# Sliding-window attention with two expert layers on one core: a new load order at the start, a new written-out order of twelve steps, and three changes of where work is done

## The chip, the cores and the metric

The kernel runs on one core of one Trainium2 chip. The metric is the device time of one execution in microseconds (us). Of the kernel before three runs were timed: 764.28, 768.56 and 769.66 us; the median is 768.56 us.

## What is computed

Inputs: q, k and v of 4 batches, 8 heads, 576 positions and 64 columns, all float32. Three stages follow each other, on 2304 tokens of 512 columns:

```
scores = q k^T / 8, kept where 0 <= i - j < 64;  x = softmax(scores) v       # attention
h = x @ w_in                               # 512 -> 2048, w_in and w_out are float64 in the input
P = a0 + a1 h + a2 h^2 + a3 h^3;  Q = 1 + |b0| |h| + |b1| h^2
y = (P / (Q + 1e-6)) @ w_out               # 2048 -> 512
e = argmax(y @ w_gate)                     # one of 8 experts per token
out = gate * sigmoid((y @ w_output_gate)[e]) * (relu(y @ w1[e]) @ w2[e])     # 512 -> 1024 -> 512
```

Products are made to near float32 accuracy: each operand is split into a rounded part and a remainder (both fp32r), and three matmuls stand for one.

## The kernel before

**Tiling.** The 2304 tokens are nine blocks of 256. Attention works on units: one block and two heads, 36 units in all. `at_T` transposes k and q of a unit on TensorE (with the identity matrix as one operand), `at_QK` makes the scores, `soften` the softmax (masks on VectorE, exponentials on ScalarE, the scaling on GpSimd), `at_PT` transposes the probabilities, `at_PV` multiplies by the values. The first three blocks do so unit by unit (`group` 1), the other six with two units at a time (`group` 2).

**The rational layer** is 72 steps, a step being one block and 256 of the 2048 columns: `rt_mm1` (24 matmuls of 256 columns, tile `h`), `rt_head`, `rt_inv`, `rt_tail` and `rt_gsplit` (the quotient, on ScalarE, VectorE and GpSimd), and four steps later `rt_mm2` (12 matmuls of 512 columns, tile `y`). The weights come in as 16 transfers of 1 MB (tile `stg`) and are converted from float64 by three VectorE operations a half (`convert`, tiles `cp` and `ct`), a copy and a subtraction.

**Routing.** After a block's last step `rt_y` writes y out, `rt_ytr` transposes it, `rt_logits` multiplies it with the gate columns (`wg`, 32 columns), `rt_logits2` transposes the result, `rt_route` picks the expert and `rt_rank` the row in the expert's list. `post` does one of these in each step.

**Expert slots.** At the end the tokens, sorted by expert, go through slots: four of 512 rows, one of 256, a half slot of 128. For each slot `w_load` brings eight tiles of 1024 columns of the expert's weights (`wr`), `w_split` rounds each (a copy, first half of `wx`) and subtracts (second half of `wx`). `slot` makes tile `hp` (first product), splits its relu into `hT` (ScalarE, then VectorE), transposes the next slot's tokens (`xtp`), and makes tile `yp` (second product).

**What sets the order.** Everything before step 12 is recorded on a tape (class `Tape`), and `play` issues it in the order written in `ORDER`: a number is the place on the tape and the letter the engine (P TensorE, A ScalarE, D VectorE, G GpSimd, S the queue of SyncE). Each engine keeps the order of its own letters. After step 12 the order comes from the tile framework's scheduler, guided by the priorities in `later`. `pick` gives an operation that two engines can do to the one with less charged work (`charge`); `arith` charges a subtraction of 1024 columns on VectorE at three times its estimate. `evs` lists what attention does in each half event.

The start of the tape: `load_qk(0)` issues q (places 2 and 3) and k (4 and 5), then one transfer brings all constants into the tile `KK` (place 6: identity, masks and small tables), then v (7 and 8), then q and k of the second pair of unit pairs (12 to 15), then the first weight tile (16).

```
    qk_upto(0)
    nc.sync.dma_start(out=cs, in_=cst[:, :C_QC + 1])
    v_upto(0)
    qk_upto(1)
    c_load(1)
```

Of the kernel before, what the change touches and what calls it, by code (L numbers as in the profile page):

```python
# [7 lines left out]
F32 = mybir.dt.float32  # L8
# [25 lines left out]

S_TAPE = 12
ORDER = (
# [32 lines left out]
)  # L69


# [58 lines left out]
def kernel(  # L130
# [89 lines left out]
    def pt(shape, name):  # L220
        return ps.tile(shape, F32, tag=name, name=name)

    def f32(ap):
        return ap.bitcast(F32)
# [26 lines left out]
    def evac(o, i, n, mul=None):  # L251
        e = pick(D=dve(n), A=act(n))
        if mul is None:
            nc.either(e, D=lambda: nc.vector.tensor_copy(out=o, in_=i), A=lambda: nc.scalar.copy(out=o, in_=i))
        else:
            nc.either(e, D=lambda: nc.vector.tensor_scalar(out=o, in0=i, scalar1=mul, scalar2=None, op0=ALU.mult),
                      A=lambda: nc.scalar.mul(out=o, in_=i, mul=mul))
# [11 lines left out]
    def mm(o, lhsT, rhs, start, stop):  # L269
        r = nc.tensor.matmul(o, lhsT, rhs, start=start, stop=stop)  # L270
        pe[0] = r and r.ins
# [34 lines left out]
    def runs(t0, n):  # L306
        done = 0
        while done < n:
            b, s = divmod(t0 + done, S)
            step = min(n - done, S - s)  # L310
            yield done, step, b, s
            done += step
# [2 lines left out]

    def load_qk(m):
        u, g = divmod(m, 2)
        for nm, src, dst in (("q", q, q_t), ("k", k, k_t)):
            dst[m] = t2([128, 2, 4, D], nm)
            for t in range(2):  # L320
                for off, n, b, s in runs(u * TB + t * 128, 128):
                    nc.sync.dma_start(
                        out=dst[m][off:off + n, t],
                        in_=src[b, 4 * g:4 * g + 4, s:s + n, :].rearrange("h p d -> p h d"),
                    )

    def load_v(m):
        u, g = divmod(m, 2)
# [289 lines left out]
        yq_t.pop(j, None)  # L618
        ysb_t[j] = ys

    yT_t, lT_t, ob_t = {}, {}, {}

    def rt_ytr(j, t):
        ys = ysb_t[j][t]
# [13 lines left out]

    def rt_logits(j, t):
        yh, yl = yT_t.pop((j, t))  # L640
        lt = pt([4 * E, 128], "lt")
        with in_turn():
            for c in range(KD):
                mm(lt, wg[:, c, :], yh[:, c, :], c == 0, False)
                mm(lt[:2 * E], wg[:, c, :2 * E], yl[:, c, :], False, c == KD - 1)
        ls = sm.tile([4 * E, 128], F32, tag="ls", name="ls")
        evac(ls, lt, 128)
        lT_t[j, t] = ls

    def rt_logits2(j, t):  # L650
        lg = pt([128, 4 * E], "lg")
        with in_turn():
            transpose(lg, lT_t.pop((j, t)))
        if t == 0:
            lg_t[j] = sm.tile([128, 2, 2 * E], F32, tag="lgs", name="lgs")
        charge("D", 0.15)
        nc.vector.tensor_reduce(out=lg_t[j][:, t, :], in_=lg.rearrange("p (x e) -> p e x", x=2), axis=AX.X, op=ALU.add)
# [198 lines left out]
    def w_split(j, x):  # L856
        t = raw_t.pop((j, x))
        w = t8([128, 2, 1024], "wx")
        r = copy(w[:, 0, :], t, 1024)
        if CH[min(j, NPRE - 1)] < NB - 1:  # L860
            tc.keep_in_program_order(r)
        arith(w[:, 1, :], t, f32(w[:, 0, :]), ALU.subtract, 1024)
        wt[j, x] = w

    def gather(j):
# [192 lines left out]
    for n in range(NUNIT + 2):  # L1058
        first, second = [], []
        if n < NUNIT and (group(n) == 1 or n % 2):  # L1060
            first.append((at_QK, n))
        if n + TA < NUNIT:
            second.append((at_T, n + TA))
        while done < min(n, NUNIT) and (group(done) == 1 or n % 2 == 0):
            first.append((at_PT, done))
            if group(done) == 1:
                second.append((at_PV, done))
            done += 1
        if n % 2 and n > 2 and group(n - 2) == 2:
            second.append((at_PV, n - 2))  # L1070
        evs += [first, second]
    assert done == NUNIT

# [20 lines left out]
    nc.on = True  # L1094
    nc.gpsimd.dma_start(out=co[:, 4:6], in_=cb.partition_broadcast(128))
    nc.gpsimd.dma_start(out=co[:, 0:4], in_=ca.partition_broadcast(128))
    qk_upto(0)
    nc.sync.dma_start(out=cs, in_=cst[:, :C_QC + 1])
    v_upto(0)
    qk_upto(1)  # L1100
    c_load(1)
# [24 lines left out]
    def post(j, r):  # L1126
        if r == 0:
            rt_ytr(j, 0)
        elif r == 1:
            rt_ytr(j, 1)  # L1130
            rt_logits(j, 0)
        elif r == 2:
            rt_logits2(j, 0)
            rt_logits(j, 1)
        elif r == 3:
            rt_logits2(j, 1)
            rt_route(j)
        elif r == RK_R:
            rt_rank(j)
# [185 lines left out]
```

## Time and profile before

| what | value |
|---|---|
| median of three runs | 768.56 us (764.28 to 769.66) |
| the profiled execution, its time | 766.85 us |
| its span (first to last instruction) | 765.1 us |
| mean granted TensorE clock | 0.989 |
| TensorE busy | 737.2 us, 96% of the span |
| VectorE, ScalarE, GpSimd busy | 505.1, 467.1, 426.9 us |
| DMA, first four fortieths of the span | 218 to 323 GB/s |

A busy engine is one with an instruction under way. For TensorE the ends are modelled and one matmul overlaps the next, so that a busy share near 100% says that it did not stand, and not that it worked at its peak. The page divides the span into 40 slices; TensorE is in its lowest slices at the start, and from then on near full until the last slice.

### The profile page before, as it was taken

What the parts mean: (1) busy time and instruction counts of PE and PEld (TensorE: products, weight loads), DVE (VectorE), ACT (ScalarE), POOL (GpSimd) and SP (SyncE); (2) the same over time, 40 slices, a digit from 0 to 9 for tenths busy, and PEclk for the clock granted to TensorE, in tenths of its full rate; (3) what the DMA queues carried; (4) which work ended last, traced back from release to release, by engine and by line L of the source; (5) the groups of instructions that cost most, each with busy time, mean ns of one, the idle gap of its engine ahead of it and who ended that gap; (6) DMA issues with size and microseconds to landing.
All of it is one profiled execution on the core that took longest, in us unless ns stands there. A gap on an engine that the chain in (4) does not pass through costs nothing. (4 is left out here: it accounts for less than half of the span.)

```text
span 765.1 us, 14765 instructions
## 1 busy us (share of the span) xinstructions
PE 737.2 (96%) x5360; PEld 646.7 (85%) x5360; DVE 505.1 (66%) x1264; ACT 467.1 (61%) x1035; POOL 426.9 (56%) x371
## 2 busy tenths in 40 slices
PE   5799999999999999999999999999999989999996
PEld 3687998899899899899899998997878878888896
DVE  4999999986869777776776767787666433224020
ACT  5799877797657757667676655675542513425131
POOL 3677776755555574565555554577644624435431
PEclk9699999999999999999999999999999999999999
DMA  9999302433222022202201002046408545311510
GB/s 218 323 256 282 108 21 84 124 101 75 57 83 56 17 64 54 57 29 57 57 28 28 3 29 83 6 134 220 165 2 274 168 143 178 134 69 54 202 44 24
DMA packets 96659, 78.57 MB, mean 103 GB/s; under 512 B 74624, under 2 KB 75008, under 8 KB 96577
## 3 DMA queue, kind: packets, MB, share of 16 engines
q1 hardware_dynamic: 92736, 67.77, 30.2%
q0 software_dynamic: 3840, 9.76, 3.7%
q8 instruction: 44, 0.72, 0.4%
q14 instruction: 39, 0.31, 0.1%
HBM read 66.25 MB, written 11.53 MB: 102 GB/s over the span
## 5 line engine op out<-in xcount | busy, mean ns | idle before, releaser
L95 PE MATMUL y<-wo,g 128*128 128x512 f32 x768 | 191.9, 397 | 0.0
L95 PE MATMUL h<-xh,wi 128*128 128x256 f32 x896 | 172.0, 284 | 1.2 <-DVE t L95 1.2
L95 PEld LDWEIGHTS y<-wo,g 128*128 128x128 f32 x768 | 139.4, 188 | 27.8 <-issue 0.7
L95 PEld LDWEIGHTS h<-xh,wi 128*128 128x128 f32 x896 | 143.7, 191 | 3.7 <-issue 1.5
L95 PE MATMUL h<-xl,wi 128*128 128x256 f32 x448 | 127.9, 285 | 0.0
L95 POOL TENSOR_TENSOR g<-t,g 128x512 fp32r<-128x512 f32 x62 | 80.2, 1293 | 52.2 <-ACT g L95 46.5
L95 PE MATMUL yp<-wx,hT 128*128 128x512 f32 x432 | 100.0, 391 | 2.2 <-DVE hT L95 2.2
L95 POOL TENSOR_TENSOR wx<-wr,wx 128x1024 fp32r<-128x1024 f32 x29 | 72.2, 2506 | 45.5 <-ACT wx L95 37.7
L95 PEld LDWEIGHTS yp<-wx,hT 128*128 128x128 f32 x432 | 80.5, 188 | 19.2 <-DVE hT L95 2.8
L95 POOL TENSOR_TENSOR qm<-qm,e 128x512 f32<-128x512 f32 x56 | 72.5, 1295 | 27.1 <-ACT qm L95 24.7
L95 PEld LDWEIGHTS h<-xl,wi 128*128 128x128 f32 x448 | 85.7, 191 | 2.3
L95 PE MATMUL hp<-xbh,wx 128*128 128x512 f32 x256 | 80.0, 390 | 0.0
L95 DVE SCALAR_TENSOR_TENSOR t<-t,KK,r 128x512 f32<-128x512 f32 x61 | 45.5, 747 | 50.1 <-ACT r L95 49.3
L95 DVE SCALAR_TENSOR_TENSOR hT<-hp,hT 128x512 fp32r<-128x512 f32 x36 | 24.4, 688 | 68.5 <-ACT hT L95 62.2
L95 ACT ACTIVATE e<-h 128x512 f32<-128x512 f32 x60 | 35.6, 594 | 54.6 <-PE h L95 40.2
L95 ACT ACTIVATE r<-qm,KK 128x512 f32<-128x512 f32 x61 | 42.1, 690 | 36.1 <-POOL qm L95 32.7
L95 DVE TENSOR_TENSOR t<-t,h 128x512 f32<-128x512 f32 x60 | 41.0, 683 | 27.6 <-ACT t L95 25.8
L95 ACT ACTIVATE ob<-yp,tl 128x512 f32<-128x512 f32 x19 | 13.0, 689 | 71.1 <-PE yp L95 64.2
L95 PEld LDWEIGHTS hp<-xbh,wx 128*128 128x128 f32 x256 | 48.0, 188 | 9.9
L95 ACT CAST g<-t 128x512 fp32r<-128x512 f32 x62 | 38.3, 618 | 27.3 <-PE h L95 9.8
L95 ACT CAST wx<-wr 128x1024 fp32r<-128x1024 f32 x44 | 44.8, 1047 | 15.7 <-PE hp L95 11.4
L95 PE MATMUL hp<-xbl,wx 128*128 128x512 f32 x128 | 50.2, 392 | 1.9 <-DVE xbl L95 1.9
(219 smaller groups left out, 1560.2 us busy)
## 6 DMA issues: line engine op xcount, KB each, us to landing
wr<-in_moe_w_dram SPq DMA_DIRECT2D x48, 512.0 KB, 4.7
stg<-in_moe_w_in_dram SPq DMA_DIRECT2D x8, 1024.0 KB, 8.2
stg<-in_moe_w_out_dram SPq DMA_DIRECT2D x8, 1024.0 KB, 7.8
v<-in_v_dram SPq DMA_DIRECT2D x58, 128.0 KB, 3.6
q<-in_q_dram SPq DMA_DIRECT2D x32, 128.0 KB, 2.7
k<-in_k_dram SPq DMA_DIRECT2D x32, 128.0 KB, 3.2
y_dram<-ysb SPq DMA_DIRECT2D x12, 256.0 KB, 3.1
yp_dram<-yq SPq DMA_DIRECT2D x6, 256.0 KB, 2.3
```

The source lines that it names most:

```text
L95: return f(*a, **k)
```

## The change

It consists of five edits. The loads of the first unit pairs are halved (two heads at a time), k goes before q, the identity is a transfer of its own, and the other constants follow after the first halves. `ORDER` is written anew; the five more transfers shift every place from 7 on by five (places 12 and 13 are now v, 17 to 20 k and q of the second pairs, 21 the first weight tile, 29P the first transposes). No operation of the tape changes its engine. `at_PV` of a two-unit group moves from the second half event of its event to the first, directly behind `at_QK`. `w_split` subtracts on GpSimd always. `rt_logits` takes y as the stationary operand and the gate columns as the moving one, so that the result needs no transpose, and `rt_logits2`, its copy to SBUF and its place in `post` go.

```diff
 ORDER = (
-    "0G 2S 3S 1G 4S 5S 6S 17G 18G 260G 7S 330G 23A 513G 8S 515G 514G 12S 516G 13S 14S 15S 16S 62S 19G "
-    "24P 21G 20G 63S 22G 11D 512G 27P 64S 25A 26D 102A 9D 65S 30P 28A 29D 93S 10A 45P 31D 87G 94S 32D "
-    "35A 33D 98S 34D 42P 36A 46D 129G 37A 47D 99S 48D 38A 59P 49D 43A 39D 44A 40D 41G 50A 69P 51A 52A "
-    "70D 165G 71D 57P 53A 72D 73D 60A 83D 107S 61A 74A 54D 109P 108S 58D 75A 76A 132S 55D 202G 84D 66P "
...
+    "7S 0G 2S 1G 5S 4S 8S 23G 26G 13S 24G 22G 25G 28A 27G 3S 265G 335G 9S 518G 517G 520G 519G 6S 521G "
+    "12S 10S 11S 107A 21S 17S 29P 20S 14D 18S 30A 32P 16D 19S 15A 31D 67S 35P 33A 34D 69S 68S 70S 50P "
+    "36D 92G 38D 40A 39D 37D 42A 88D 99S 41A 134G 51D 43A 98S 54D 52D 55A 53D 104S 56A 44D 89D 57A 103S "
...
     def load_qk(m):
         u, g = divmod(m, 2)
-        for nm, src, dst in (("q", q, q_t), ("k", k, k_t)):
+        for nm, dst in (("k", k_t), ("q", q_t)):
             dst[m] = t2([128, 2, 4, D], nm)
...
+        step = 4 if m else 2
+        for h0 in range(0, 4, step):
+            for src, dst in ((k, k_t[m]), (q, q_t[m])):
+                for t in range(2):
+                    for off, n, b, s in runs(u * TB + t * 128, 128):
+                        h = 4 * g + h0
+                        nc.sync.dma_start(out=dst[off:off + n, t, h0:h0 + step],
+                                          in_=src[b, h:h + step, s:s + n, :].rearrange("h p d -> p h d"))
+            if m == 0 and h0 == 0:
+                nc.sync.dma_start(out=cs[:, C_MASK:], in_=cst[:, C_MASK:C_QC + 1])
...
     def rt_logits(j, t):
         yh, yl = yT_t.pop((j, t))
-        lt = pt([4 * E, 128], "lt")
+        lg = pt([128, 4 * E], "lg")
         with in_turn():
             for c in range(KD):
-                mm(lt, wg[:, c, :], yh[:, c, :], c == 0, False)
-                mm(lt[:2 * E], wg[:, c, :2 * E], yl[:, c, :], False, c == KD - 1)
-        ls = sm.tile([4 * E, 128], F32, tag="ls", name="ls")
-        evac(ls, lt, 128)
-        lT_t[j, t] = ls
-
-    def rt_logits2(j, t):
-        lg = pt([128, 4 * E], "lg")
-        with in_turn():
-            transpose(lg, lT_t.pop((j, t)))
+                mm(lg, yh[:, c, :], wg[:, c, :], c == 0, False)
+                mm(lg[:, :2 * E], yl[:, c, :], wg[:, c, :2 * E], False, c == KD - 1)
...
-        arith(w[:, 1, :], t, f32(w[:, 0, :]), ALU.subtract, 1024)
+        charge("G", pool(1024))
+        nc.gpsimd.tensor_tensor(out=w[:, 1, :], in0=t, in1=f32(w[:, 0, :]), op=ALU.subtract)
...
         if n < NUNIT and (group(n) == 1 or n % 2):
             first.append((at_QK, n))
+        if n % 2 and n > 2 and group(n - 2) == 2:
+            first.append((at_PV, n - 2))
...
-        if n % 2 and n > 2 and group(n - 2) == 2:
-            second.append((at_PV, n - 2))
...
+    nc.sync.dma_start(out=ident, in_=cst[:, C_ID:C_ID + 128])
     qk_upto(0)
-    nc.sync.dma_start(out=cs, in_=cst[:, :C_QC + 1])
...
         elif r == 2:
-            rt_logits2(j, 0)
             rt_logits(j, 1)
         elif r == 3:
-            rt_logits2(j, 1)
             rt_route(j)
```

## Rows read from the trace of the kernel before

**Rows 1.** Windows: us of stretch, busy per engine, granted clock, DMA share, GB/s.

```profile
0.00:60.00 60.00, 44.93 (x505) 37.67 (x506) 48.06 (x171) 46.02 (x151) 36.65 (x53) 0.89 0.99 269
60.00:140.00 80.00, 77.65 (x570) 69.74 (x569) 79.14 (x162) 63.98 (x137) 57.65 (x49) 1.00 0.38 115
140.00:500.00 360.00, 360.00 (x2991) 325.11 (x2990) 265.39 (x722) 250.59 (x589) 206.89 (x190) 1.00 0.20 54
500.00:765.00 265.00, 254.65 (x1300) 214.19 (x1298) 112.47 (x211) 106.54 (x160) 125.70 (x82) 0.99 0.38 128
```

**Rows 2.** Waits of TensorE: whom it waited for, us in total, times, longest.

```profile
PE tq L123 <- DMA KK<-in_const_dram: 7.6, 1, 7.6
PE xp L123 <- ACT ms L123: 2.7, 3, 1.2
PE yp L95 <- DVE hT L95: 2.2, 1, 2.2
...
PE hp L95 <- DVE xbl L95: 1.9, 1, 1.9
PE tq L123 <- DMA k<-in_k_dram: 1.9, 1, 1.9
```

**Rows 3.** Timeline, first 16 us: start, us, engine, operation, count, idle before.

```profile
0.86 1.00 SPq L123 DMA_DIRECT2D q<-in_q_dram  x2
...
3.00 0.51 SPq L123 DMA_DIRECT2D KK<-in_const_dram  x1
...
7.61 0.66 PE L123 MATMUL tq<-KK,k 128*128 128x128 f32 x2 [7.61 <-DMA KK<-in_const_dram]
...
7.86 0.50 SPq L123 DMA_DIRECT2D stg<-in_moe_w_in_dram  x1
...
9.70 1.98 PE L123 MATMUL sc<-KK 64*64 64x128 f32 x32 [0.16 <-DVE KK L123]
...
15.90 0.69 DVE L123 TENSOR_SCALAR cp<-stg 128x512 uint32<-128x512 uint32 x1
```

**Rows 4.** Transfers of the page: KB each, median us from issue to landing.

```profile
q<-in_q_dram SPq DMA_DIRECT2D x32, 128.0 KB, 2.7
```

**Rows 5.** Timeline of TensorE, the first two steps of the rational layer.

```profile
34.71 4.50 PE L123 MATMUL h<-x,wi 128*128 128x256 f32 x24
...
42.53 3.12 PE L123 MATMUL h<-x,wi 128*128 128x256 f32 x24
```

**Rows 6.** Timeline of TensorE around one tile of logits, at 305 us.

```profile
305.68 0.28 PE L95 MATMUL h<-xh,wi 128*128 128x256 f32 x1
305.88 0.24 PE L95 MATMUL lg<-KK,ls 32*128 32x32 f32 x1
306.06 0.25 PE L95 MATMUL lt<-yh,wg 128*32 128x128 f32 x1
...
306.56 0.39 PE L95 MATMUL tq<-KK,k 128*128 128x128 f32 x2
```

**Rows 7.** Tile views (ns min/median/max): weight loads of 32, 16 and 128 columns, subtractions.

```profile
L95 PEld LDWEIGHTS lt<-yh,wg x72: 106/108/165, 186.0 to 555.7; 128*32 128x32 f32 x72
...
L95 PEld LDWEIGHTS lt<-yl,wg x72: 93/96/103, 186.6 to 555.8; 128*16 128x16 f32 x72
...
L95 PEld LDWEIGHTS hp<-xbh,wx x256: 186/188/192, 530.0 to 700.3; 128*128 128x128 f32 x128
...
L95 POOL TENSOR_TENSOR wx<-wr,wx x29: 2369/2398/3493, 505.9 to 737.2; 128x1024 fp32r<-128x1024 f32 x29
...
L95 DVE TENSOR_TENSOR wx<-wr,wx x15: 1219/1226/7736, 537.6 to 740.0; 128x1024 fp32r<-128x1024 f32 x15
```

**Rows 8.** Timeline at 605 us, between the first and second product of a slot.

```profile
605.12 9.44 POOL L95 TENSOR_TENSOR wx<-wr,wx 128x1024 fp32r<-128x1024 f32 x4
...
607.91 7.74 DVE L95 TENSOR_TENSOR wx<-wr,wx 128x1024 fp32r<-128x1024 f32 x1 [4.16 <-ACT wx L95]
...
615.57 1.27 DVE L95 SCALAR_TENSOR_TENSOR hT<-hp,hT 128x512 fp32r<-128x512 f32 x2
```

More of the change, by code (lines that the diff above doesn't have):

```diff
@@ L317, in load_qk @@
         u, g = divmod(m, 2)
-        for nm, src, dst in (("q", q, q_t), ("k", k, k_t)):
+        for nm, dst in (("k", k_t), ("q", q_t)):
             dst[m] = t2([128, 2, 4, D], nm)
[L320 to L325, printed above, removed]
+        step = 4 if m else 2
[8 more added lines that the diff above has]
+                nc.sync.dma_start(out=cs[:, C_MASK:], in_=cst[:, C_MASK:C_QC + 1])
     def load_v(m):
@@ L619, in rt_y @@
         ysb_t[j] = ys
-    yT_t, lT_t, ob_t = {}, {}, {}
+    yT_t, ob_t = {}, {}
     def rt_ytr(j, t):
```

58 rows, old and new, of the table ORDER are left out of this document.

## The prediction

> **What bounds the kernel now.** I read the stages first, by windows [rows 1]. Between 140 and 500 us TensorE is busy for all of 360 us, so there the time is the sum of its matmuls and nothing else. From 500 us on it is free for 265.0 - 254.65 = 10.35 us. In the first 60 us it is free for 15.07 us, in the next 80 for 2.35. The same rows show what stands against it at the start: VectorE is busy 79.14 of 80 us from 60 to 140, and in the first 60 us the transfers hold 0.99 of all DMA engines. So the start is a matter of transfers and VectorE, the middle of TensorE's work, the end of single waits.
>
> Next come TensorE's waits [rows 2]. The largest is the first: 7.6 us until the constants, and with them the identity, have landed. Two waits of the slots add up to 4.1 us (2.2 for `hT`, 1.9 for `xbl`). The other three rows, and smaller ones, are attention at the start, while VectorE and ScalarE feed it.
>
> **1. Loads and the order of the start.** Today the constants are the fifth transfer of SyncE, issued at 3.00 us; the first is issued at 0.86 [rows 3], so one issue takes 2.14 / 4 = 0.535 us. TensorE starts at 7.61, that is 4.6 us after the issue. In the new order the queue's letters are 7, 2, 5, 4, 8, 13, 3, 9, 6, 12, 10, 11, 21: the masks go first, the identity second, but the first transposes need places 3 to 6 as well, and place 6 is the ninth transfer, issued at 0.86 + 8 x 0.535 = 5.1 us. The second unit's transposes (32P, still ahead of the first scores, 35P) need place 11, the twelfth: 6.7 us. With 4.6 us to landing it is there at 11.3, with the page's median of 2.7 us for such a transfer [rows 4] at 9.4. The evacuation and the rest took the scores from 7.61 to 9.70 [rows 3] for two units; for the last half unit I take 0.8 us. The scores then start between 10.2 and 12.1 instead of 9.70: 0.5 to 2.4 us later, not sooner. The identity's own transfer buys nothing, since q becomes the last to land.
>
> The five more issues also move the queue: the first weight tile is the thirteenth transfer (it was the twelfth, at 7.86), at 7.3 us, ahead of the second pairs' q and k. It took 8.0 us from issue to its conversion at 15.90 [rows 3], so it is there at 15.3. The new order puts that conversion (88D) right behind the first unit's four masks; VectorE, in order, then stands before it, and the second unit's masks (51D) behind it. Against that, the conversions come sooner in VectorE's list, and the first products of the rational layer (34.71 us [rows 5]) can come sooner too.
>
> What can the order win? At most TensorE's waits in the first 140 us other than the first: 15.07 + 2.35 - 7.6 = 9.8 us. The low clock adds a little: the first 24 matmuls of the layer took 4.50 us, the next 3.12 [rows 5], in a stretch whose clock is granted at 0.89 on the mean [rows 1], so partly at 1.2 and not 2.4 GHz: 1.4 us. What can it lose? The 2.4 us above, and as much again where VectorE stands: +4. VectorE's work on the tape is the same, it has hardly a gap from 60 to 140 us, and 60 - 48.06 = 11.9 us free before; most of that is before the first data. So the order can save far less than 9.8. I take -2.5 us, bounds -10 and +4.
>
> **2. Logits with swapped operands.** Removed for each of 18 tiles is the transpose `lg`: it starts 0.20 us after an `h` matmul and the next starts 0.18 later [rows 6], while an `h` matmul alone takes 3.12 / 24 = 0.13 [rows 5], so it costs 0.25 us. The eight matmuls of `lt` take 0.50 us (306.06 to 306.56 [rows 6]). Added are eight matmuls with only 32 or 16 moving columns, but with y as weights: 128 columns to load in place of 32 or 16. No row shows such a matmul. Bounds: 0.0625 us each as now (0.50 for eight) and 0.13 as an `h` matmul, which loads 128 columns too (1.04). Which end is near? The weight loads last 94 ns (16 columns, mean of the row's 93 and 96), 107 (32) and 188 (128) [rows 7]; that is (188 - 94) / 112 = 0.84 ns a column, so 128 columns occupy the loading path for 107 ns, and short matmuls hide none of it behind moving columns. I take 0.11: eight make 0.88. Net 0.88 - 0.50 - 0.25 = +0.13 us a tile, 18 tiles +2.3 us; bounds -4.5 and +5.2. All of it lies where TensorE is full, so it is on the path. The copy of `ls` that goes was on ScalarE, which is not the bound after 140 us (250.59 of 360): nothing.
>
> The Trainium skill, page "TensorE: Matmul & The Clock Gate", section "LDWEIGHTS (loading the stationary operand)", gives columns / 1.2 ns, which agrees with the slope above; but its section "Wait — 56ns, not 53.3ns?" has 25 ns as the least distance of two small matmuls, by which eight would take 0.2 us and the sum of this edit would be -9.9 us. Both are the page's; the rows speak for the first.
>
> **3. Value products next to scores.** The same matmuls in another place. A change of tile shape costs some 0.07 us (0.20 in place of 0.13 before `lg` [rows 5, 6]); twelve pairs save at most one such change each: -1.0 us, bounds -1.0 and +0.5 (a pair whose probabilities are a half event late; their transposes are issued an event earlier, which covers it). I take -1.0.
>
> **4. Subtractions on GpSimd.** Fifteen leave VectorE; GpSimd gets fifteen of 2.4 us [rows 7], 36 us, beside the 125.70 of 265 us that it is busy in the last stage [rows 1]. The cover is its free half; each slot needs eight, 19 us. The last slots have the least room: GpSimd's last one starts at 737.2 [rows 7], ends by 739.6, and the half slot's work is all that then remains. What goes is one wait with a clear cause [rows 8]: VectorE's subtraction at 607.91 lasts 7.74 us, not 1.23 (its median [rows 7]), and ends 1.1 us after GpSimd's four in a row (605.12 to 614.56); the `hT` behind it starts at 615.57, and TensorE's 2.2 us [rows 2] are that. With no such subtraction left on VectorE it is gone: -2.2. The wait for `xbl` (1.9) has another operation of VectorE in front of it; it stays. Bounds: -4.1 (both go) and +10.9 (the last rival). VectorE's charge falls, so `pick` may hand it copies of weights instead, which stand behind GpSimd in the same way.
>
> **The sum**: -2.5 + 2.3 - 1.0 - 2.2 = -3.4 us. The profiled execution took 766.85 us (span 765.1), 1.7 under the median of 768.56; I set the sum on the median: 765.2.
>
> **The rivals.** (B) The order closes the gaps of the start: its term is -9.8, the sum -10.7, 757.9 us. For it: single waits of 1 to 2 us for ScalarE, GpSimd and a k transfer [rows 2] are what an order can mend. Against it: VectorE has no room. (C) The first part doesn't do what it says, since q lands last and VectorE stands before the weights: +4 in place of -2.5, sum +3.1, 771.7 us. (D) Slower: copies of weights go to VectorE and stand behind GpSimd's rows of subtractions, and `hT` with them, at each of the five passages from one slot to the next. It decides from a blockage of 7.74 - 2.2 = 5.5 us on, more than two subtractions of 2.4 in a row; each passage then costs 2.2, together 10.9 in place of -2.2, sum +9.7, 778.3 us. For it: one such row of four is there [rows 8]; against it: one passage only shows the wait today, and ScalarE made all the copies. The Trainium skill, page "SBUF — State Buffer", section "Who interferes with whom", says that VectorE and GpSimd lock a shared pair of ports for a whole instruction, copies among them; the 7.74 us agree. (E) Loading weights is hidden: eight short matmuls cost 0.50 us, the logits -4.5 in place of +2.3, sum -10.2, 758.4 us. Against it the 188 ns of the loads [rows 7].
>
> **How the numbers follow.** Chances: forecast 0.47, B 0.25, C 0.10, D 0.08, E 0.10. A measurement of this kernel can tell about 1% (7.7 us) from no change: faster is below 760.9, slower above 776.3. B and E are faster (0.35), the forecast and C within 1% (0.57), D slower (0.08). The forecast's own range is 761 to 770; the one stated, 756 to 772, takes in B, E and C and leaves out D and the tails.
>
> **What would show it.** First scores after 10 us show the loads right; before 9 they are wrong. TensorE's free time in the first 140 us, now 17.4, shows the order's term: about 15 by the forecast, under 9 by B, 20 or more by C. Eight matmuls of `lg` within 0.8 to 1.0 us show the logits; 0.5 or less is E. A wait of `yp` for `hT` gone, and no new one at a passage, shows the subtractions; VectorE copies of `wx` of several us show D. The prediction is wrong if the middle stage, steps 12 to the first slot, changes by more than 4 us in either direction: nothing in my sum does that.

## The result, and the profile after

The changed kernel takes 758.9 us (median, 757.36 to 761.39) beside 768.14 us for the kernel before on the same chip: ratio 0.9886, 95% interval 0.9859 to 0.9912, so 1.1% faster. That lies 6.3 us under the predicted 765.2. The profiled executions are 759.05 us (span 757.4) and 766.85 us (span 765.1), and the rest of the document finds out where these 7.7 us of span went.

The four windows of [rows 1], now for the changed kernel:

```profile
0.00:60.00 60.00, 43.58 (x522) 36.27 (x524) 48.64 (x177) 47.49 (x154) 37.29 (x53) 1.00 0.95 257
60.00:140.00 80.00, 77.78 (x571) 68.86 (x566) 78.01 (x160) 64.37 (x138) 58.08 (x49) 1.00 0.43 133
140.00:500.00 360.00, 359.36 (x2976) 327.58 (x2975) 270.44 (x719) 251.40 (x577) 206.02 (x188) 1.00 0.20 54
500.00:765.00 265.00, 251.30 (x1285) 213.72 (x1283) 117.34 (x222) 82.10 (x128) 158.41 (x95) 0.99 0.40 125
```

The granted clock of the first 60 us rose from 0.89 to 1.00. In the last stage GpSimd has more to do, since it makes all the subtractions, and ScalarE less (106.54 to 82.10 us), since `pick` hands VectorE some copies of weights. Windows of fixed length mislead about when work is done, though: a faster clock alone makes TensorE look idler. So I compare the start times of the same work in the two timelines (us):

| work | before | after | difference |
|---|---|---|---|
| first product of the rational layer, step 0 | 34.7 | 32.8 | -1.9 |
| step 1 | 42.5 | 36.6 | -6.0 |
| step 8 | 89.2 | 87.8 | -1.5 |
| step 16 | 137.9 | 136.1 | -1.8 |
| step 68 | 496.8 | 494.3 | -2.5 |
| slot 0, first product (`hp`) | 530.2 | 527.8 | -2.4 |
| slot 0, second product (`yp`) | 563.3 | 558.8 | -4.5 |
| slot 1, first product | 585.9 | 580.6 | -5.3 |
| slot 2, first product | 633.7 | 626.0 | -7.7 |
| end of the span | 765.1 | 757.4 | -7.7 |

Read downwards, the last column says where time was won: 1.8 us up to step 16, 0.6 from there to step 68, 5.2 from step 68 to slot 2 (1.84, 0.62 and 5.25 before rounding), and nothing afterwards. The 4.1 us between step 0 and step 1 are hardly a gain: in the kernel before TensorE makes 44 matmuls of attention between the two steps, in the changed kernel four. The rest come behind step 1:

```profile
36.57 3.12 PE L124 MATMUL h<-x,wi 128*128 128x256 f32 x24
39.62 0.69 PE L124 MATMUL xp<-ms,v 128*64 128x64 f32 x16
...
42.98 3.14 PE L124 MATMUL h<-x,wi 128*128 128x256 f32 x24 [1.22 <-DVE ct L124]
```

So steps 1 to 8 take 51.2 us instead of 46.7. Of these 4.5 us, 3.4 are the attention work that was put there, and 1.1 are longer waits of TensorE (3.0 us, 2.8 of them for VectorE, beside 1.9 before).

TensorE's waits in the changed kernel, to be read beside [rows 2]:

```profile
PE tq L124 <- DMA k<-in_k_dram: 10.7, 4, 7.4
PE pp L124 <- POOL ms L124: 2.3, 2, 1.2
PE h L96 <- DVE mn L96: 1.5, 1, 1.5
PE h L124 <- DVE ct L124: 1.2, 1, 1.2
```

Both waits of the slots are gone, the one for `hT` (2.2) that I had counted out, and the one for `xbl` (1.9) that I had said would stay. Every remaining wait of half a microsecond or more lies in the first 140 us.

The start, beside [rows 3]:

```profile
6.95 0.47 SPq L124 DMA_DIRECT2D stg<-in_moe_w_in_dram  x1
...
7.36 0.66 PE L124 MATMUL tq<-KK,k 128*128 128x128 f32 x2 [7.36 <-DMA k<-in_k_dram]
...
9.46 1.98 PE L124 MATMUL sc<-KK 64*64 64x128 f32 x32 [0.16 <-DVE KK L124]
...
13.23 0.69 DVE L124 TENSOR_SCALAR cp<-stg 128x512 uint32<-128x512 uint32 x1 [1.57 <-DMA stg<-in_moe_w_in_dram]
```

The scores start at 9.46 instead of 9.70; I had said after 10, and by my signs (after 10 right, before 9 wrong) that settles nothing. The first conversion starts at 13.23 instead of 15.90 (I had said 15.3), and VectorE stands 1.57 us before it, as foretold.

One tile of logits, beside [rows 6]:

```profile
303.16 0.28 PE L96 MATMUL h<-xh,wi 128*128 128x256 f32 x1
303.28 0.18 PE L96 MATMUL lg<-wg,yh 128*128 128x32 f32 x1
303.31 0.26 PE L96 MATMUL lg<-wg,yl 128*128 128x16 f32 x1
303.42 0.26 PE L96 MATMUL lg<-wg,yh 128*128 128x32 f32 x1
...
304.09 0.87 PE L96 MATMUL pp<-KK,ms 128*128 128x128 f32 x6
```

Eight matmuls take 304.09 - 303.28 = 0.81 us, most of them 0.11 apart: rival E (0.50 or less) is out.

### The profile page after: what moved, and what is told of

Same layout as the page of the kernel before. It is cut to its first block, busy times and chain, and to the rows that moved or that the text cites. A ratio compares the mean times of both kernels' runs of the same rounds, so it can differ in the third digit from the quotient of the medians.

```text
span 757.4 us, 14698 instructions
## 1 busy us (share of the span) xinstructions
PE 732.0 (97%) x5342; PEld 646.4 (85%) x5342; DVE 514.4 (68%) x1275; ACT 445.4 (59%) x994; POOL 459.8 (61%) x383
## 5 line engine op out<-in xcount | busy, mean ns | idle before, releaser
L96 POOL TENSOR_TENSOR wx<-wr,wx 128x1024 fp32r<-128x1024 f32 x44 | 107.4, 2464 | 27.5 <-DVE wx L96 10.0
L96 ACT ACTIVATE ob<-yp,tl 128x512 f32<-128x512 f32 x12 | 8.3, 690 | 78.9 <-PE yp L96 63.4
L96 ACT ACTIVATE hT<-hp 128x512 fp32r<-128x512 f32 x36 | 21.3, 596 | 50.3 <-PE hp L96 47.4
```

Source lines behind the costliest of these rows:

```text
L96: return f(*a, **k)
```

## The experiments

The ratio is to the kernel before on the same chip. "Waits" are those of TensorE for `hT` and `xbl` in the slots; "16 to 68" is the time from the start of step 16 to that of step 68 (358.9 before, 358.3 in the changed kernel). All but the ratio are from one profiled execution each. A new `ORDER` by itself lengthens this stretch to 360.1 us, although each kernel makes the same number of matmuls of each tile in it (but for `lt` and `lg`), so rows with the new `ORDER` are compared with each other only.

| kernel | ratio (interval) | waits hT, xbl | 16 to 68 |
|---|---|---|---|
| before, again | 1.0007 (0.9984 to 1.0031) | 2.0, 1.0 | 358.9 |
| before + subtractions on GpSimd | 0.9976 (0.9954 to 0.9998) | 0, 1.9 | 358.9 |
| before + logits | 0.9944 (0.9924 to 0.9964) | 0, 0 | 359.3 |
| before + value products | 0.9960 (0.9939 to 0.9981) | 0, 0 | 359.6 |
| before + loads and order | 0.9984 (0.9960 to 1.0008) | 0, 1.4 | 360.1 |
| before + loads | 1.0043 (1.0023 to 1.0063) | 2.2, 2.1 | 358.9 |
| before + order | 0.9986 (0.9967 to 1.0004) | 2.3, 1.8 | 360.1 |
| after - subtractions | 0.9882 (0.9852 to 0.9912) | 0, 0 | 358.1 |
| after - logits | 0.9914 (0.9884 to 0.9943) | 0, 0 | 361.3 |
| after - value products | 0.9902 (0.9884 to 0.9919) | 0, 0 | 360.5 |
| after, queue in order of need | 0.9919 (0.9901 to 0.9936) | 0, 0 | 359.5 |
| the same, copies of v later | 0.9897 (0.9880 to 0.9914) | 0, 0 | 358.4 |

**Each edit by itself, on the kernel before.** First the subtractions:

```diff
-        arith(w[:, 1, :], t, f32(w[:, 0, :]), ALU.subtract, 1024)
+        charge("G", pool(1024))
+        nc.gpsimd.tensor_tensor(out=w[:, 1, :], in0=t, in1=f32(w[:, 0, :]), op=ALU.subtract)
```

> The kernel before with one edit: the fifteen subtractions of slot weights that VectorE did go to GpSimd. Theory 1 (VectorE standing behind GpSimd is the cause of both waits of TensorE in the slots): both waits, 2.2 us for hT and 1.9 us for xbl, are gone and the time falls by 4 to 5 us. Theory 2 (only the hT wait hangs on these subtractions; the xbl wait went in the changed kernel because other edits shifted the work): 2 to 2.5 us less, with a wait of TensorE for xbl of 1 to 2 us still there. Theory 3 (weight copies that move to VectorE stand behind GpSimd and make hT late): a new wait of TensorE for hT of 2 us or more at some passage between slots, and no gain.

Measured: the wait for `hT` went and that for `xbl` stayed at 1.9, just as I had priced it, and TensorE's order is that of before, instruction by instruction. The time fell by 1.7 us (764.51 beside 766.24), a little less than theory 2 has. Taken alone, this run would have confirmed the step. Then the logits (`rt_logits2` goes with it):

```diff
...
-                mm(lt, wg[:, c, :], yh[:, c, :], c == 0, False)
...
+                mm(lg, yh[:, c, :], wg[:, c, :], c == 0, False)
...
```

> The kernel before with one edit: logits with swapped operands. Theory 1 (the load of 128 weight columns sets the pace of the eight matmuls, 0.11 us each, and removing the transpose pays back 0.26 us): slower by 1 to 2.5 us. Theory 2 (interleaved with transposes of other tiles and followed by matmuls whose load is hidden, the eight cost about what the old pair cost): within 0.7 us of no change. Theory 3 (loads are hidden): 4 us faster or more.

Measured: the time fell by 4.0 us (762.23 beside 766.24), as theory 3 has it, but not for its reason. The middle grew by 0.4 us; what went are both waits, although VectorE still does 15 subtractions. Then the value products:

```diff
...
+            first.append((at_PV, n - 2))
...
-            second.append((at_PV, n - 2))
...
```

> The kernel before with one edit: value products of two-unit groups directly behind the scores. Theory 1 (a change between tiled and full matmuls costs TensorE some 0.09 us on entering and up to 0.16 us on leaving, and twelve pairs save one such change each): 1 to 2.5 us faster. Theory 2 (changes of shape cost nothing that is not hidden by a weight load): within 0.5 us of no change. Theory 3 (the products come before their probabilities are ready): slower, with waits of TensorE for the probabilities in the stage from 140 to 500 us.

Measured: the time fell by 3.1 us (763.09 beside 766.24), and again both waits vanished; the middle grew by 0.7, with 1.2 of new waits of `ytp` for VectorE. From 515 us on the sequence of every engine is that of before, so here the waits went by a shift in time alone. Last, loads and `ORDER` together, of which the diff stands ahead of the prediction:

> The kernel before with one edit: the new loads and the new written order of the first twelve steps. Theory 1 (the start is worth what the seventeenth step shows in the two traces, 136.1 against 137.9 us): 1.5 to 2.5 us faster, and the start's granted clock stays at 1.00. Theory 2 (the start is worth more, as the first products of the second layer, 60.8 against 66.2 us, say, and the other edits gave part of it back): 4 us faster or more. Theory 3 (the start alone gives nothing, since VectorE bounds the first 140 us): within 0.7 us of no change.

Measured: step 16 is 3.7 us sooner, steps 24 to 68 2.5, and the wait for `hT` is gone here too. The median fell by 1.2 us only (765.05 beside 766.24; the interval reaches no change), between theories 1 and 3; the profiled execution, 761.65 us, lies 3.4 under it. From 165 us on every engine's sequence is that of before. So three edits that leave the slots' subtractions alone take away the wait that I had put down to them. The theory "the subtraction on VectorE costs 2.2 us" falls as a cause; it is one condition of several.

**Is the wait a thing of the program at all?** The kernel before, unchanged:

> The kernel before, unchanged, profiled and timed a second time. Theory 1 (the two waits of the slots belong to the order of its program): TensorE waits 2.2 us for hT and 1.9 us for xbl again, each within 0.3 us, and VectorE's subtraction near 608 us lasts over 7 us again. Theory 2 (they are accidents of one execution): at least one of them is gone or changed by over 1 us. The ratio is 1.000 by both, within 0.002. The low clock at the start was 13.7 us in the first profile, and 3.4 to 13.7 in the four single edits' profiles; if it belongs to the program it is 13.7 again, if it varies between executions it is anything from 0 to 14.

Measured: `hT` 2.0 and `xbl` 1.0; VectorE's subtraction lasts 7.58 us, at 608.21. The `hT` wait is reproducible; the `xbl` wait shrank by 0.9, since TensorE came to it 1.3 us later and the last `xbl` only 0.3. The low clock at the start was 13.7 us again (in the four single edits 6.8 to 13.7, not from 3.4 on). The start itself moved: step 16 came 1.3 us later than in the first profile, in the same program, so a difference of that size in a single profile of the start says nothing.

**Undoing one edit of the changed kernel**, by the same diffs reversed. The subtractions given back to either engine:

> The changed kernel with its subtractions of wx given to either engine as before. Theory 1, as the prediction has it (subtractions on VectorE cause the wait for hT, and GpSimd removes it): the wait of some 2.2 us comes back, 761 us, ratio to before 0.991 to 0.995. Theory 2 (any edit that alters the order of GpSimd's subtractions removes it): no wait for hT, and the time is that of the changed kernel within 1 us, 758 to 760, ratio 0.988 to 0.990.

Measured: 759.7 us, ratio 0.9882 beside 0.9886, no wait for `hT`. Theory 1 falls: in the changed kernel this edit is worth nothing. The old logits:

> The changed kernel with the logits as before (gate columns stationary, result transposed). Theory 1, the prediction's price (0.88 us for eight swapped matmuls, +0.13 us a tile): faster than the changed kernel by 1 to 3 us, 756 to 758, from steps 16 to 68 by 1 to 2 us. Theory 2 (the swapped form costs the same or less where it stands beside other matmuls): the middle stage within 0.5 us, the whole within 1 us of the changed kernel or slower, ratio to before 0.988 to 0.992.

Measured: 762.29 us, 2.6 more than the 759.70 of the run before, which was timed with it. Theory 1 falls, and theory 2 with its middle stage too: from step 16 to 68 it took 361.3 us, 3.0 *more* than the changed kernel. Of these, 2.2 are longer waits (2.8 for `mn`, `t` and `ms` beside 0.6), 0.8 is matmuls. So where the value products stand next to the scores the swapped logits do not cost 1 to 2 us, they save 0.8, and 3.0 with the waits. The value products moved back:

> The changed kernel with the value products of the later blocks in the second half event, as before. Theory 1 (the move saves one change of tile shape for each of ten pairs, as the prediction has it, and the sum of its term holds where the logits are swapped too): from step 16 to step 68 it takes 1.0 us longer than the changed kernel, 0.5 to 1.7, and 760 us in all. Theory 2 (the edits don't add: the move cost 0.7 us there when it was made alone): 0.7 us or more shorter than the changed kernel.

Measured: 762.67 us, ratio 0.9902, and 360.5 from 16 to 68, 2.3 more than the changed kernel, although it waits less there (0.2 us beside 0.6). The sign is theory 1's, the size is beyond its range. The edits don't add. On the old order, 358.9 us in the middle, the logits alone cost 0.4 us and the value products alone 0.7. On the new one, 360.1 us (loads and order), they cost 0.4 (the row "after - value products") and 1.2 ("after - logits"), and both together save 1.8; the subtractions don't enter (358.1 without them).

**Loads or order?** The new loads with the old order of the computation:

```diff
...
+    nc.sync.dma_start(out=ident, in_=cst[:, C_ID:C_ID + 128])
     qk_upto(0)
-    nc.sync.dma_start(out=cs, in_=cst[:, :C_QC + 1])
...
```

> The kernel before with the new loads alone: k before q, halves, the identity by itself, issued in the sequence of the code with the identity first, and the written-out order of everything else as before. Theory 1 (the loads bring the gain of the start): first scores before 9.5 us, the rational layer's steps 1 to 16 earlier by 2 us or more. Theory 2 (the order of the computation brings it, and the loads alone bring nothing or cost up to 2 us because weights are issued five transfers later): the first scores may be earlier, yet step 16 is within 1 us of before or later; ratio 0.996 to 1.003.

Measured: 0.4% slower; every step from the second on 4.5 us later. The first weight tile is issued at 9.77 us instead of 7.86, and VectorE stands for it:

```profile
17.86 0.69 DVE L125 TENSOR_SCALAR cp<-stg 128x512 uint32<-128x512 uint32 x1 [1.99 <-DMA stg<-in_moe_w_in_dram]
```

This is the second half of rival C's mechanism (VectorE stands before the weights), near its price (+4), in a kernel that issues the transfers in the sequence of the code. TensorE's own first matmul came at 3.39 us and the scores at 9.57, which helped nothing.

Next comes the new order with the old loads. The expectation says that the loads keep the sequence of before; they don't. `ORDER` holds the queue's letters too, and the first weight tile is issued at 4.57 us, ahead of q and k of the second pairs. So this run does not separate the order of the computation from that of the queue.

> The kernel before with the new written-out order of the computation alone; the loads are those of before, in their sequence. Seen so far: loads and order together start step 16 3.7 us sooner, the loads alone 4.5 us later. Theory 1 (the two need each other: the new order puts VectorE's first conversion early because the new queue brings the weights early): step 16 is within 1 us of before, ratio 0.994 to 1.002. Theory 2 (the order alone makes the gain, the loads only cost): step 16 is 2.5 us or more sooner than before. By both the wait for hT goes, as after every edit that altered the order of the slots.

Measured: step 16 2.3 us sooner (just short of theory 2's 2.5), of which 1.0 is left at step 24; no gain in time. And I was wrong on what I took for settled: both waits of the slots are there again (2.3 and 1.8). This kernel and "loads and order" differ in the slots in nothing but timing: every engine's rows stand in the same sequence in the two, and in the kernel before. That made the pair worth a closer look (next section).

**Could the start be better?** The changed kernel with the first thirteen places of the queue sorted by need:

```diff
-    "7S 0G 2S 1G 5S 4S 8S 23G 26G 13S 24G 22G 25G 28A 27G 3S ... 9S ... 6S ... 12S 10S 11S ... 21S ...
+    "2S 3S 4S 5S 6S 7S 8S 9S 10S 11S 21S 13S 12S 0G 1G 23G 26G 24G 22G 25G 28A 27G ...
...
+    "... 36D 92G 38D 40A 39D 37D 14D 16D 42A 88D ...
```

> The changed kernel with its first thirteen transfers in the sequence in which the first units need them (identity, k and q of the first two heads, masks, k and q of the next two, first weight tile, v), and VectorE's two copies of v behind the first unit's masks. Theory 1 (the start waits for what lands last, as the prediction has it): TensorE's first transposes start before 6 us, the first scores before 8.7, the first conversion 0.5 to 1.3 us before the 13.23 of the changed kernel, and steps 8 to 68 are sooner by 0.5 to 1.5 us. Theory 2 (from step 8 on the start is set by VectorE's total work and by the transfers' sum, not by the first scores): the first scores come sooner but step 16 is within 0.5 us of the changed kernel.

Measured: 763.96 us. TensorE's first matmul came at 3.42, but the scores at 13.55: I had left two copies of v on ScalarE ahead of the evacuation, and they now stood for the later v (idle 7.64 us). A failed edit, but it prices lateness: scores 4.1 us later than in the changed kernel made step 8 4.4 later and the end 5.0. With those two copies moved as well (`107A` and `15A` behind `41A`):

> The changed kernel with the queue in the sequence of need, as the run before it, but ScalarE's two copies of v are moved behind the first unit's exponentials as well, so that no engine stands for v before the first scores. Everything else is the changed kernel's order. Theory 1 (what the start reaches first carries through: first scores 4.1 us later made step 8 4.5 us later): first scores at 8.3 to 8.8, first conversion at 11.5 to 12.7, steps 8 to 16 sooner than the changed kernel by 0.7 to 1.5 us, 757 to 758.5 us, ratio 0.984 to 0.988. Theory 2 (the transfers' sum sets the rest): the scores come sooner but steps 8 to 16 are within 0.5 us or later, ratio 0.988 to 0.991.

Measured: 760.70 us, ratio 0.9897. The scores came at 8.09, 1.4 us before those of the changed kernel, and step 8 came 1.9 us *later*. Theory 1 falls. VectorE now stood 3.18 us for v, just ahead of the first conversion:

```profile
13.49 0.72 DVE L125 COPY v<-v 64x512 f32<-64x512 f32 x2 [3.18 <-DMA v<-in_v_dram]
14.13 0.68 DVE L125 TENSOR_SCALAR cp<-stg 128x512 uint32<-128x512 uint32 x1
```

Side by side (us; the last column is step 12 against the kernel before):

| kernel | first scores | first conversion | step 12 |
|---|---|---|---|
| before | 9.70 | 15.90 | 0 |
| before + loads | 9.57 | 17.86 | +4.5 |
| loads and order | 9.55 | 12.78 | -2.1 |
| after | 9.46 | 13.23 | -1.4 |
| after, queue in order of need | 13.55 | 16.43 | +3.0 |
| the same, copies of v later | 8.09 | 14.13 | +0.4 |
| before + order | 9.55 | 12.34 | -0.6 |

Within one order of the computation (rows 3 to 6) step 12 follows the first conversion, not the first scores. How finely this can be read is seen in the three undo runs, whose start is the changed kernel's: conversions at 12.79 to 13.04 us go with -1.2 to -0.4. The last row breaks the line: there q and k of the second pairs come late. None of these versions beats the changed kernel.

## Why the prediction came out as it did

| term, us | predicted | profiled executions |
|---|---|---|
| start, to step 16 | -2.5 | -1.84 |
| middle, to step 68: logits (14 tiles), value products | +0.8 | -0.62 |
| slots: wait for `hT`, logits (4 tiles) | -1.7 | -5.25 |
| sum | -3.4 | -7.71 |

The medians are 9.2 us apart, 1.5 more, most of it because the profiled execution of before was itself 1.3 us under its median. So the likeliest case fell short of half the gain, and the 0.35 that I gave to a gain over 1% went to two rivals that did not happen. The measured 758.9 us lies in the stated range of 756 to 772 but under the forecast's own, 761 to 770. It lies in the stated one because room was left there for B and E, for neither of their reasons: that is luck.

**The two waits of the slots, the largest part (5.2 us, where my terms gave some 1.7 there: -2.2 for `hT`, +0.5 for the last four tiles of logits).** The 5.2 us are 1.9 for `xbl`, 2.2 for `hT`, 0.8 in slot 0 (below) and 0.4 whose cause is open. The wait for `xbl` was mis-sorted: I wrote that it "has another operation of VectorE in front of it; it stays". That operation is the same collision. In the kernel before, VectorE's rows, TensorE's, and GpSimd's beside them:

```profile
526.91 4.26 DVE L95 SCALAR_TENSOR_TENSOR cd<-cd,KK 128x16 f32<-128x16 f32 x1
...
532.41 0.68 DVE L95 TENSOR_TENSOR xbl<-xtp,xbh 128x512 fp32r<-128x512 f32 x1
...
533.14 0.50 PE L95 MATMUL hp<-xbl,wx 128*128 128x512 f32 x1 [1.90 <-DVE xbl L95]
...
527.49 2.39 POOL L95 TENSOR_TENSOR wx<-wr,wx 128x1024 fp32r<-128x1024 f32 x1
529.84 1.29 POOL L95 TENSOR_TENSOR g<-t,g 128x512 fp32r<-128x512 f32 x1
```

An operation on 16 columns that otherwise takes 0.17 us lasts 4.26, to the end of GpSimd's two; the last `xbl` stands behind it, and TensorE behind that. `cd` belongs to the routing of the block. With the swapped logits that routing runs at 522 us, ahead of the products' `xbl`:

```profile
522.64 0.17 DVE L96 SCALAR_TENSOR_TENSOR cd<-cd,KK 128x16 f32<-128x16 f32 x1
...
524.78 1.88 DVE L96 TENSOR_TENSOR xbl<-xtp,xbh 128x512 fp32r<-128x512 f32 x3
...
527.25 0.68 DVE L96 TENSOR_TENSOR xbl<-xtp,xbh 128x512 fp32r<-128x512 f32 x1
```

There the logits edit gave what I hadn't looked for: not less work on TensorE but a transpose and a copy fewer in the chain from y to the expert's list. The last maximum of logits (`lgs`) is at 545.8 us instead of 560.9, and at 549.3 with the logits edit alone. Slot 0 itself (from `yp` to the next `hp`) is 0.8 us shorter in each kernel with that edit, and the same as before within 0.2 in the others; the cause of that is open.

The logits edit is not the only way, though: the run without it ("after - logits") has no wait for `xbl` either. The value products alone show how. VectorE's sequence is that of before, but the collision comes earlier and falls on `d`, three operations ahead of `cd`:

```profile
525.26 3.84 DVE L95 TENSOR_TENSOR d<-lgs,mx 128x16 f32<-128x16 f32 x1
...
531.11 0.68 DVE L95 TENSOR_TENSOR xbl<-xtp,xbh 128x512 fp32r<-128x512 f32 x1
...
531.84 0.50 PE L95 MATMUL hp<-xbl,wx 128*128 128x512 f32 x1
```

It ends some 2 us sooner (529.1 instead of 531.2), and the last `xbl` starts 0.7 us before TensorE comes for it. So this wait, too, is a matter of when the two engines meet.

**The wait for `hT`: right in its place, wrong in its cause.** Three rows decide. GpSimd in the kernel before, up to the four subtractions of [rows 8]:

```profile
597.79 1.02 POOL L95 DMA_INDIRECT out_dram<-ob,tl  x1 [0.30 <-issue]
604.11 0.99 POOL L95 DMA_INDIRECT out_dram<-ob,tl  x1 [5.30 <-DMA out_dram<-ob,tl]
```

and with loads and order alone, where GpSimd's sequence is the same:

```profile
593.64 1.03 POOL L97 DMA_INDIRECT out_dram<-ob,tl  x1 [0.30 <-issue]
597.88 1.00 POOL L97 DMA_INDIRECT out_dram<-ob,tl  x1 [3.22 <-DMA wr<-in_moe_w_dram]
598.89 2.43 POOL L97 TENSOR_TENSOR wx<-wr,wx 128x1024 fp32r<-128x1024 f32 x1
604.18 8.09 POOL L97 TENSOR_TENSOR wx<-wr,wx 128x1024 fp32r<-128x1024 f32 x3 [2.85 <-ACT wx L97]
```

VectorE beside it:

```profile
605.08 2.57 DVE L97 TENSOR_TENSOR wx<-wr,wx 128x1024 fp32r<-128x1024 f32 x1 [4.16 <-ACT wx L97]
607.57 1.28 DVE L97 SCALAR_TENSOR_TENSOR hT<-hp,hT 128x512 fp32r<-128x512 f32 x2
```

In the kernel before GpSimd issues one scatter of output rows and stands 5.30 us before the next; when it goes on, all four subtractions are ready and run in a row for 9.44 us, and VectorE, which comes in the midst of them, gets its turn at the end. In the other kernel the second scatter goes 4.2 us after the first and not 6.3; one subtraction is done early, and VectorE's, 0.9 us after the start of the next run of three, gets in after the first (8.09 is 0.9 more than three times 2.4). Six profiles have this sequence on every engine in the slots. In the four that show the wait, the interval between the two scatters is 6.1 to 6.4 us; in the other two (loads and order, value products) it is 4.2 and 4.8. So the wait came with a late second scatter, next to the weights' transfers of 0.5 MB; that the one causes the other is read from these rows and not tested, which of the transfers holds the scatter up isn't separated, and whether the wait comes back in other executions isn't shown: with loads and order the profiled execution took 761.65 us, its median 765.05.

The wait can also cost more than its 2.2 us. In two of the four profiles (loads alone, order alone), behind TensorE's standing still the granted clock is at the lower of its two levels for 3.4 us: 0.57 on the mean from 622 to 626 us in the first, 0.82 from 612 to 618 in the second. From the `yp` that waits to the next `hp` these two take 26.0 us, the other two 24.3 and 24.2, and the changed kernel 21.9.

The Trainium skill, page "SBUF — State Buffer", section "Who interferes with whom", says that VectorE and GpSimd share a pair of ports as an exclusive lock, and of VectorE's two-port modes that the engine which issues first holds the pair for its whole instruction while the other one blocks. The rows agree that it blocks, tiny operations too. Who issued first they don't settle: the row of `cd` starts 0.58 us before GpSimd's subtraction, and still VectorE stands. They add that it may block for several instructions of the other in a row (7.74 us beside a row of four of 2.4, or 2.57 for one), on what condition no run here shows.

**Rival D's mechanism did occur**, at no price. VectorE makes 18 of the 44 copies of `wx`, and one met three subtractions:

```profile
560.49 7.99 DVE L96 CAST wx<-wr 128x1024 fp32r<-128x1024 f32 x1
...
560.83 7.09 POOL L96 TENSOR_TENSOR wx<-wr,wx 128x1024 fp32r<-128x1024 f32 x3
```

The first is VectorE's row, the second GpSimd's. It falls in slot 0 behind the second product's start, where no `hT` was due; I had placed it "at each of the five passages".

**The logits' term (+2.3) was mis-sized by the neighbours.** The price of the new form was good: 0.81 us for eight where I took 0.88. What failed was the price of the old form: 0.50 for eight came from one tile without neighbours. Summed over the 14 tiles between steps 16 and 68, from each start to the next, `lt` and `lg` took 12.5 us before, 0.89 a tile and not 0.75, since in ten of the 14 `lt` was cut up by other matmuls (by `pp` in six). With the edit alone `lg` took 11.1, but `pp` and `tq` together 18.0 instead of 15.8, and the other tiles 0.4 less; the middle came out 0.4 us longer, where 14 tiles of +0.13 gave 1.8.

**Value products (-1.0)**: +0.7 alone (-0.5 without its new wait), -2.3 within the changed kernel. The bounds -1.0 and +0.5 were too narrow on both sides. A change of tile shape costs more than the 0.07 us that I read: from the last matmul of one shape to the first of the other it is 0.20 us, both from scores straight to value products in the changed kernel and from `tq` to value products before, where one `tq` follows another after 0.11; what goes is one return from scores to full tiles of 0.20 a pair. Why the gain is there only beside the swapped logits is open.

**The start (-2.5)** was the right size: -1.8 at step 16 in the profiled executions, and over five profiles with the old start (137.8 to 139.2, mean 138.5) and five with the new one (134.2 to 136.3, mean 135.7) -2.8. But two of its steps failed. The scores were not 0.5 to 2.4 us late: one issue took 0.51 and not 0.535 us, so place 11 was issued at 6.4, and it had landed by 8.7 us, 2.2 later, where I had taken 2.7 to 4.6. And "free time of TensorE" was a bad yardstick: it went from 17.4 to 18.6 while the start got shorter, because the same 1056 matmuls up to step 16 kept TensorE busy for 117.5 us and not 120.5. A gain by the clock doesn't show behind step 0: in the profiled execution 13.7 us at the lower of the two levels went to none, and step 0 took 3.54 instead of 4.50 us, but the five profiles with the new start spent 0 to 10.2 us at that level and reach step 8 in no order of it (87.8 and 88.8 us with none, 87.2 and 88.0 with 6.8, 88.8 with 10.2).

**The yardstick for the middle** held: from step 12 to the first slot it took 417.5 us instead of 418.5, a change of 1.0, under the 4 that would have sunk the sum. Rivals B and E have times near the result (757.9, 758.4), but B's free time under 9 us and E's 0.50 us did not come.

## What to carry to other kernels

Where VectorE and GpSimd share a stage, look in the timeline for short VectorE operations with long durations. Those shown here all ended with GpSimd's rows beside them, and which of them cost something was decided by what stood behind them and when, not by which operation it was. Before an edit is given the credit for a wait that goes, run another edit that should leave the wait alone. In a start that one engine limits, as VectorE does here, order the loads by when that engine gets its first long work, not by when TensorE gets its first matmul; four rows of the table of starts are all that shows it.

## What the runs showed that was not expected

Edits that don't touch each other's work interact by 1 to 3 us through the order of the matmuls: the logits cost 0.4 us in the middle alone and saved some 0.8 (3.0 with waits) in the changed kernel. A short VectorE operation was held up to 25 times its length (4.26 instead of 0.17 us) by GpSimd. And two executions of one program differ by 1.3 us at step 16, of which 0.2 is left at the end, since the waits of the slots take up the rest.
